# One attention-and-experts kernel: the tail queries' values as five full 128x128 products, and their inverse sums taken after the product

## The chip, the core and the metric

The kernel runs on one core of one Trainium2 chip. The metric is the device time of one execution in microseconds (us). The engines are named as in the profile: PE (matrix products; PEld its weight loads), DVE (VectorE), ACT (ScalarE), POOL (GpSimd) and SP, which issues most DMAs.

## What is computed

Rotary attention over 2 batches, 8 heads, 576 positions and head size 64, whose output feeds a dense mixture of 4 experts (all float32):

```python
q_rot, k_rot = (rotate(q), rotate(k))                 # q, k, v: 2 x 8 x 576 x 64
scores = scale * np.matmul(q_rot, k_rot.transpose(0, 1, 3, 2))
scores = scores - np.max(scores, axis=-1, keepdims=True)
attn = np.exp(scores)
attn = attn / (np.sum(attn, axis=-1, keepdims=True) + 1e-09)
x = np.matmul(attn, v)                                # then to 1152 x 512
for e in range(4):                                    # w1: 512 x 1024, w2: 1024 x 512
    out += p[:, e:e + 1] * (np.maximum(x @ w1[e], 0.0) @ w2[e])
```

## The kernel before

A `Pair` is two heads of one batch. Their 576 queries are 9 blocks: blocks 0 to 3 are the 512 main queries of the first head, 4 to 7 those of the second, and block 8, the **tail**, holds the last 64 queries of both heads, one head under the other on the 128 partitions. Per block the kernel makes scores (line 282), their row maxima (293, DVE), exponentials with row sums (301, ACT), transposes of the exponentials on PE in four pieces of 128 keys (315) and one of the last 64 keys (341), and copies of them out of PSUM.

Main blocks: the transposed exponentials are split into a high and a low float32r part (332 on ACT, 336 on DVE, 344 and 348 for the last keys), multiplied by the split values (365 to 368), and the two halves of the product are added (372 ACT, 376 DVE). When a head pair is complete its inverse sums (382, 383, DVE) are spread over a tile `rep` (392), turned on PE (398), and the product is multiplied by them (403). `out_high` (406, ACT) and `out_low` (410, POOL; DVE for the very last pair) write the two parts that the experts read.

The tail: DVE multiplies all 128x576 exponentials of block 8 by the inverse sums first (387); then come the transposes, ACT copies the four pieces to `at` (351), DVE the last 64 keys (354), and `tail_values` (417) multiplies them by the raw values: for each head five products of 64x64, the last over 64 keys only. ACT (426) and DVE (430) split the result.

The raw values of a pair lie in `rawv` by head (line 159); a pair's load is one DMA for the main rows of both heads (162) and two for the tail rows (170). `split_v` makes the float32r parts. `swap_halves` (first pair only) keeps a copy `lh` of k in the buffer of `at`.

The order of all this work is written as numbers: the dictionaries `ALONE` (first batch, attention alone) and `BESIDE` (second batch, beside the experts) give each step of a block a time in units of blocks, `place` (432) puts it on the agenda, and `plan.run()` issues everything in that order; each engine executes its own list in order. In the first batch there are two sets of buffers and PSUM banks; near its end `narrow` leaves one, and the four pairs of the second batch run between the matmuls of the experts on the first 512 tokens (601 to 603 first layer, 576 to 578 second). Behind them come the experts on the remaining 640 tokens (737 to 739, 822 to 824), whose inputs the `Quarters` steps combine from all pairs' results (644 to 660).

Of the kernel before, what the change touches and what calls it, by code (L numbers as in the profile page):

```python
# [26 lines left out]
    copy_x=2.409, inverse=0.587, scale=0.712, spread=3.143, rows=4.075, divide=4.404, out_high=8.561,  # L27
    out_low=9.259, tail_values=4.354, tail_high=4.658, tail_low=4.771,
# [4 lines left out]
    tail_turn_x=1.122, copy_x=1.44, inverse=0.243, scale=0.697, spread=0.555, rows=2.195, divide=2.503,  # L33
    out_high=9.813, out_low=10.683, tail_values=2.033, tail_high=2.528, tail_low=2.554,
# [21 lines left out]
def kernel(  # L56
# [21 lines left out]
    P = 128  # L78
# [66 lines left out]
    class Pair:  # L145
# [9 lines left out]
        def load(self, s, queue=nc.sync, heads=((0, 2),)):  # L155

            hp, nm = self.hp, self.nm
            src = {"k": k, "q": q, "v": v}[s]
            x = self.pool.tile([P, 2, NS, D], F32, tag=f"raw{s}", name=f"raw{s}{nm}")
            hs = src[self.b, 2 * hp : 2 * hp + 2]  # L160
            for i, (a, z) in enumerate(heads):
                queue.dma_start(
                    out=x[:, a:z, 0:NR, :], in_=hs[a:z, 0:SM, :].rearrange("h (p r) d -> p h r d", r=NR)
                )
                if i:
                    continue
                for j in range(2):
                    rows = slice(j * ST, (j + 1) * ST)
                    if s == "v":
                        queue.dma_start(out=x[rows, :, NR, :], in_=hs[:, SM:S, :].rearrange("h p d -> p h d"))  # L170
                    else:
                        queue.dma_start(out=x[rows, 0, NR, :], in_=hs[j, SM:S, :])
            self.raw[s] = x
# [28 lines left out]
        def split_v(self, eng_h=nc.gpsimd, eng_l=nc.gpsimd):  # L202
            self.vs = self.pool.tile([P, 2, NS, 2, D], F32R, tag="vs", name=f"vs{self.nm}")
            split(eng_h, eng_l, self.raw["v"], self.vs[:, :, :, 0, :], self.vs[:, :, :, 1, :])
# [105 lines left out]
        def turn_e(self, u):  # L310
# [6 lines left out]
            if u == TAIL:  # L317
                self.at = apool.tile([P, NS, P], F32, tag="at", name=f"at{nm}")
# [31 lines left out]
        def copy_e(self):  # L350
            nc.scalar.activation(out=self.at[:, 0:NR, :], in_=self.et.pop(TAIL), func=AF.Copy)

        def copy_x(self):
            nc.vector.tensor_copy(self.at[0:ST, NR, :], px[:, 0:P])
# [46 lines left out]

        def divide(self):
            nc.vector.tensor_tensor(out=self.xf, in0=self.xf, in1=self.pr, op=ALU.mult)
# [4 lines left out]
        def out_low(self):  # L408
            eng = nc.vector if (self.b, self.hp) == (B - 1, NP - 1) else nc.gpsimd
            eng.tensor_tensor(out=self.dst[1], in0=self.xf, in1=f32(self.dst[0]), op=ALU.subtract)  # L410

        def tail_values(self):
            po = self.po = banks["x"].pick()[:, 2 * P : 2 * P + ST]
            for j in range(2):
                for c in range(NS):
                    n = P if c < NR else ST
                    nc.tensor.matmul(  # L417
                        po[j * D : (j + 1) * D, :],
                        lhsT=self.raw["v"][0:n, j, c, :],
                        rhs=self.at[0:n, c, j * ST : (j + 1) * ST],  # L420
                        start=(c == 0),
                        stop=(c == NR),
                    )

        def tail_high(self):
            nc.scalar.activation(out=self.tail_dst[0], in_=self.po, func=AF.Copy)

        def tail_low(self):
            cH, cL = self.tail_dst
            nc.vector.tensor_tensor(out=cL, in0=self.po, in1=f32(cH), op=ALU.subtract)  # L430

        def place(self, u, t, step, o):
# [8 lines left out]
            if u == TAIL:  # L441
                at("tail_turn", self.turn_e, u)
                at("tail_turn_x", self.turn_x, u)
                for key in (
                    "copy_e", "copy_x", "inverse", "scale", "spread", "rows", "divide", "out_high", "out_low",
                    "tail_values", "tail_high", "tail_low",
# [429 lines left out]
    apool = attn.enter_context(tc.tile_pool(name="apool", bufs=1, side="right"))  # L876
    evens, odds = pools("pair")
# [11 lines left out]
    for x in qTt:  # L889
        nc.gpsimd.memset(f32(x), 0.0)  # L890
# [232 lines left out]
```

## Time and profile before

| | |
|---|---|
| three runs, median | 574.27 us (572.32 to 576.47) |
| the profiled execution's own time | 573.63 us |
| its span, first to last instruction | 571.8 us |
| mean granted clock | 0.997 |
| PE, DVE, ACT, POOL busy | 95%, 57%, 49%, 59% of the span |

"Busy" of PE counts pipelined records from start to modelled end, so it doesn't mean full speed. The first batch's attention lies between 8 and 105 us, the second batch's attention beside the experts up to 358, the experts on the last 640 tokens behind that.

### The profile page before, as it was taken

Reading aid. Unit: us, or ns where it says so; the run is one execution under the profiler, and the core shown is the slowest. Engines: PE = TensorE matmul, PEld = TensorE weight load, DVE = VectorE, ACT = ScalarE, POOL = GpSimd, SP = SyncE. Lnnn points to the kernel's source line nnn. Section 1 sums busy time; section 2 is a strip of 40 time slices with the busy share of each in tenths; the row PEclk is TensorE's granted clock in tenths of the full one; section 3 lists DMA queues with packets and bytes.
Section 4 is the critical chain, followed back from the end, with each engine's and each line's share of the span. In section 5 each row is a group of like instructions: output and inputs, shape, how many; then the busy total and the mean of one; then the engine's idle time right before and its main releaser. Section 6 shows DMA issues by size and latency. Waiting matters only on the chain.

```text
span 571.8 us, 8611 instructions
## 1 busy us (share of the span) xinstructions
PE 545.8 (95%) x3229; PEld 478.5 (84%) x3229; DVE 325.4 (57%) x586; ACT 277.8 (49%) x545; POOL 337.5 (59%) x232
## 2 busy tenths in 40 slices
PE   4898988999999999999999998999999999999996
PEld 3788877888888888888888886998899899889985
DVE  5588898234362434444334435995578658757702
ACT  5678888365444544556436552554154225324500
POOL 7999965458824673379244388458663664565400
PEclk9999999899999999999999999999999999999999
DMA  5245023054224222442242222631323213223102
GB/s 151 70 115 136 18 56 97 18 172 153 73 62 156 73 75 54 121 120 70 76 104 79 66 75 76 222 107 38 109 78 100 65 57 111 75 73 78 72 0 92
DMA packets 42459, 50.67 MB, mean 89 GB/s; under 512 B 7218, under 2 KB 32050, under 8 KB 42418
## 3 DMA queue, kind: packets, MB, share of 16 engines
q1 hardware_dynamic: 41618, 49.38, 29.1%
q10 hardware_dynamic: 800, 0.75, 0.5%
q8 instruction: 25, 0.41, 0.3%
q14 instruction: 16, 0.13, 0.1%
HBM read 43.34 MB, written 2.36 MB: 80 GB/s over the span
## 4 chain that ended last, share of the span: by engine, by line
PE 78%; DVE 7%; ACT 7%; POOL 4%; issue 2%; DMA 1%; SPq 0%; ACTq 0%; POOLq 0%; DVEq 0%
PE po L824 6%; PE po L822 6%; PE po L823 6%; PE p L737 6%; PE p L739 5%; PE p L738 5%; PE sc L282 5%; PE ph L601 4%; PE ph L603 4%; PE ph L602 4%; PE po L578 4%; PE po L576 4%; PE po L577 4%; PE pp L315 4%; ACT e L301 3%; PE x L417 3%
## 5 line engine op out<-in xcount | busy, mean ns | idle before, releaser
L142 POOL TENSOR_TENSOR wl<-wr,wh 128x1024 fp32r<-128x1024 f32 x64 | 154.3, 2412 | 145.6 <-ACT wh L135 144.1
L135 ACT ACTIVATE wh<-wr 128x1024 fp32r<-128x1024 f32 x64 | 67.2, 1052 | 28.8 <-PE po L578 16.7
L293 DVE TENSOR_REDUCE mx<-sc 128x1 f32<-128x576 f32 x72 | 54.2, 752 | 37.7 <-PE sc L282 37.3
L301 ACT ACTIVATE e<-sc,mx 128x576 f32<-128x576 f32 x72 | 53.3, 740 | 22.1 <-DVE mx L293 21.6
L142 POOL TENSOR_TENSOR sl<-sf,sh 128x1024 fp32r<-128x1024 f32 x16 | 38.5, 2404 | 42.5 <-ACT sh L135 42.5
L824 PE MATMUL po<-wh,hL 128*128 128x512 f32 x160 | 62.3, 389 | 0.0
L823 PE MATMUL po<-wl,hH 128*128 128x512 f32 x160 | 62.3, 389 | 0.0
L822 PE MATMUL po<-wh,hH 128*128 128x512 f32 x160 | 62.3, 389 | 0.0
L562 DVE SCALAR_TENSOR_TENSOR hL<-ph,hH 128x512 fp32r<-128x512 f32 x32 | 22.1, 692 | 61.1 <-ACT hH L561 61.1
L576 PE MATMUL po<-wh,hH 128*128 128x512 f32 x128 | 52.3, 409 | 0.0
L601 PE MATMUL ph<-xH,wh 128*128 128x512 f32 x128 | 51.5, 402 | 0.0
L315 PE MATMUL pp<-ident,e 128*128 128x128 f32 x288 | 45.3, 281 | 5.9 <-DVE e L387 3.4
L332 ACT ACTIVATE ptH<-pp 128x512 fp32r<-128x512 f32 x64 | 38.1, 595 | 25.1 <-PE x L365 17.3
L578 PE MATMUL po<-wh,hL 128*128 128x512 f32 x128 | 50.3, 393 | 0.0
L336 DVE TENSOR_TENSOR ptL<-pp,ptH 128x512 fp32r<-128x512 f32 x64 | 43.9, 686 | 11.1 <-ACT ptH L332 10.8
L603 PE MATMUL ph<-xH,wl 128*128 128x512 f32 x128 | 50.1, 392 | 0.0
L577 PE MATMUL po<-wl,hH 128*128 128x512 f32 x128 | 50.0, 391 | 0.0
L602 PE MATMUL ph<-xL,wh 128*128 128x512 f32 x128 | 50.0, 391 | 0.0
L135 ACT ACTIVATE sh<-sf 128x1024 fp32r<-128x1024 f32 x16 | 16.9, 1059 | 67.1 <-DVE sf L516 67.1
L775 ACT ACTIVATE hH<-p 128x320 fp32r<-128x320 f32 x64 | 27.1, 435 | 40.3 <-DVE p L767 40.3
L315 PEld LDWEIGHTS pp<-ident,e 128*128 128x128 f32 x288 | 34.3, 143 | 12.2 <-issue 2.0
L516 DVE TENSOR_TENSOR sf<-wr 128x256 f32<-128x256 f32 x30 | 32.2, 1114 | 17.4 <-DMA wr<-in_moe_w_dram 17.4
(164 smaller groups left out, 1375.3 us busy)
## 6 DMA issues: line engine op xcount, KB each, us to landing
wr<-in_moe_w_dram SPq DMA_DIRECT2D x68, 512.0 KB, 3.6
k2T<-kT SPq DMA_DIRECT2D x14, 288.0 KB, 4.1
rawv<-in_v_dram SPq DMA_DIRECT2D x8, 256.0 KB, 3.1
out_dram<-acc SPq DMA_DIRECT2D x8, 256.0 KB, 2.5
rawk<-in_k_dram SPq DMA_DIRECT2D x7, 256.0 KB, 4.1
rawq<-in_q_dram SPq DMA_DIRECT2D x7, 256.0 KB, 3.0
rawv<-in_v_dram SPq DMA_DIRECT2D x16, 32.0 KB, 2.6
tabs<-in_rope_dram ACTq DMA_DIRECT2D x1, 320.0 KB, 3.5
```

The lines of the kernel that those rows point to most:

```text
L135: nc.scalar.activation(out=hi, in_=src, func=AF.Copy)
L142: eng_l.tensor_tensor(out=lo, in0=src, in1=f32(hi), op=ALU.subtract)
L315: nc.tensor.transpose(pp[:, c * P : (c + 1) * P], self.e[u][:, c * P : (c + 1) * P], ident)
L576: nc.tensor.matmul(po[t], lhsT=sH, rhs=wH, start=(f == 0), stop=False)
L577: nc.tensor.matmul(po[t], lhsT=sH, rhs=wL, start=False, stop=False)
L578: nc.tensor.matmul(po[t], lhsT=sL, rhs=wH, start=False, stop=(f == NF - 1))
L601: nc.tensor.matmul(o, lhsT=wH[:, kt], rhs=xh, start=(kt == 0), stop=False)
L602: nc.tensor.matmul(o, lhsT=wH[:, kt], rhs=xl, start=False, stop=False)
L603: nc.tensor.matmul(o, lhsT=wL[:, kt], rhs=xh, start=False, stop=(kt == KT1 - 1))
L822: nc.tensor.matmul(po[t], lhsT=sH, rhs=wH, start=(f == 0), stop=False)
L823: nc.tensor.matmul(po[t], lhsT=sH, rhs=wL, start=False, stop=False)
L824: nc.tensor.matmul(po[t], lhsT=sL, rhs=wH, start=False, stop=(f == NF - 1))
```

## The change

The tail's exponentials are no longer multiplied by the inverse sums. Instead the raw values lie with both heads side by side (`rawv` becomes keys x piece x head x 64), so that one product of 128 value columns by 128 query columns does both heads; of its four 64x64 blocks the two on the diagonal are used. Five such float32 products replace ten. The last one reads `tail_keys`, a 128x128 tile whose lower 64 rows are set to zero once at the start. The tail's inverse sums are turned on PE as a broadcast column (`tail_rows`), ACT keeps the two 64x64 blocks (`keep_tail_rows`), and DVE multiplies the product by them (`tail_divide`). The low part of the tail goes to POOL, as the main part's does. Each load of values is now one DMA per head, with pieces of 64 numbers in SBUF. `lh` moves to another buffer.

```diff
 ALONE = dict(
...
-    copy_x=2.409, inverse=0.587, scale=0.712, spread=3.143, rows=4.075, divide=4.404, out_high=8.561,
-    out_low=9.259, tail_values=4.354, tail_high=4.658, tail_low=4.771,
+    copy_x=2.409, inverse=0.587, spread=3.143, rows=4.075, divide=4.404, out_high=8.561,
+    out_low=9.259, tail_rows=1.6, keep_tail_rows=2.405, tail_values=4.354, tail_divide=4.658, tail_high=4.659, tail_low=4.771,
 )
...
+            if s == "v":
+                x = self.pool.tile([P, NS, 2, D], F32, tag="rawv", name=f"rawv{nm}")
+                for j in range(2):
+                    queue.dma_start(out=x[:, 0:NR, j, :], in_=hs[j, 0:SM, :].rearrange("(p r) d -> p r d", r=NR))
+                for j in range(2):
+                    rows = slice(j * ST, (j + 1) * ST)
+                    queue.dma_start(out=x[rows, NR], in_=hs[:, SM:S, :].rearrange("h p d -> p h d"))
...
-            self.lh = apool.tile([P, NS, P], F32R, tag="at", name=f"lh{self.nm}")
+            self.lh = odds.tile([P, NS, P], F32R, tag="vs", name=f"lh{self.nm}")
...
-            nc.vector.tensor_copy(self.at[0:ST, NR, :], px[:, 0:P])
+            nc.vector.tensor_copy(tail_keys[0:ST], px[:, 0:P])
...
-        def scale(self):
-            e = self.e[TAIL]
-            nc.vector.tensor_scalar_mul(e, e, self.total[:, TAIL:])
...
+        def tail_rows(self):
+            self.prt = xb[1][:, 0:P] if banks["x"].n > 1 else xb[0][:, 3 * P : 4 * P]
+            nc.tensor.transpose(self.prt, self.total[:, TAIL:].to_broadcast([P, P]), ident)
+
+        def keep_tail_rows(self):
+            self.xt = apool.tile([P, ST], F32, tag="xt", name=f"xt{self.nm}", bufs=2)
+            for rows, cols in self.blocks():
+                nc.scalar.activation(out=self.xt[rows], in_=self.prt[rows, cols], func=AF.Copy)
+
+        def blocks(self):
+            return [(slice(j * D, (j + 1) * D), slice(j * ST, (j + 1) * ST)) for j in range(2)]
...
         def tail_values(self):
-            po = self.po = banks["x"].pick()[:, 2 * P : 2 * P + ST]
-            for j in range(2):
-                for c in range(NS):
-                    n = P if c < NR else ST
-                    nc.tensor.matmul(
-                        po[j * D : (j + 1) * D, :],
-                        lhsT=self.raw["v"][0:n, j, c, :],
-                        rhs=self.at[0:n, c, j * ST : (j + 1) * ST],
...
+            po = self.po = banks["x"].pick()[:, 2 * P : 3 * P]
+            for c in range(NS):
+                nc.tensor.matmul(
+                    po,
+                    lhsT=self.raw["v"][:, c].rearrange("p h d -> p (h d)"),
+                    rhs=self.at[:, c, :] if c < NR else tail_keys,
...
+        def tail_divide(self):
+            for rows, cols in self.blocks():
+                nc.vector.tensor_tensor(
+                    out=self.xt[rows], in0=self.po[rows, cols], in1=self.xt[rows], op=ALU.mult
+                )
 
         def tail_high(self):
-            nc.scalar.activation(out=self.tail_dst[0], in_=self.po, func=AF.Copy)
+            nc.scalar.activation(out=self.tail_dst[0], in_=self.xt, func=AF.Copy)
 
         def tail_low(self):
             cH, cL = self.tail_dst
-            nc.vector.tensor_tensor(out=cL, in0=self.po, in1=f32(cH), op=ALU.subtract)
+            self.spare_engine().tensor_tensor(out=cL, in0=self.xt, in1=f32(cH), op=ALU.subtract)
...
+    tail_keys = apool.tile([P, P], F32, name="tail_keys")
...
-    for x in qTt:
+    for x in (*qTt, tail_keys):
         nc.gpsimd.memset(f32(x), 0.0)
```

Two places in the order show what moves. First PE in the last pair of the second batch, between the matmuls of the experts' second layer (`po`); `x_112` and `x_113` are the same PSUM bank, `at` and `tail_keys` the transposed exponentials, `pr` the main rows' inverse sums. Before:

```order
L578 MATMUL po_3_3_3675<-wh_3_1_2_3496,hL_3_5_3567 128x512
L417 MATMUL x_112<-at_3_8_3860,rawv_3_3340 64x64 x10
L398 MATMUL pr_3_3901<-ident,rep_3_3830 128x128 x4
L576 MATMUL po_3_0_3672<-wh_3_1_3_3572,hH_3_6_3608 128x512
L577 MATMUL po_3_0_3672<-wl_3_1_3_3573,hH_3_6_3608 128x512
```

And now, with the changed kernel's own line numbers:

```order
L600 MATMUL po_3_3_3685<-wh_3_1_2_3506,hL_3_5_3577 128x512
L407 MATMUL x_113<-ident,total_3_3399 128x128
L430 MATMUL x_113<-at_3_8_3869,rawv_3_3347 128x128 x4
L430 MATMUL x_113<-tail_keys,rawv_3_3347 128x128
L401 MATMUL pr_3_3909<-ident,rep_3_3840 128x128 x4
L598 MATMUL po_3_0_3682<-wh_3_1_3_3582,hH_3_6_3618 128x512
```

Ten products became five of twice the width, and the transpose of the inverse sums stands in front of them. Second, DVE in the same pair, from the inverse sums to the `Quarters` step (`s`); `xt` is the tail's result. Before:

```order
L383 RECIPROCAL total_3_3389<-total_3_3389 128x9
L348 TENSOR_TENSOR ptX_3_6_3737<-x_112,ptX_3_6_3737 64x256
L392 COPY rep_3_3830<-total_3_3389 128x512
L387 TENSOR_SCALAR e_3_8_3804<-e_3_8_3804,total_3_3389 128x576
L354 COPY at_3_8_3860<-x_112 64x128
L376 TENSOR_TENSOR xf_3_3536<-x_112,tmp_3_3_3869 64x256
L403 TENSOR_TENSOR xf_3_3536<-xf_3_3536,pr_3_3901 128x512
L430 TENSOR_TENSOR xL_76<-x_112,xH_74 128x64
L410 TENSOR_TENSOR xL_76<-xf_3_3536,xH_74 128x512
L644 TENSOR_TENSOR s_3926<-xH_74,xL_76 128x320
```

And now:

```order
L390 RECIPROCAL total_3_3399<-total_3_3399 128x9
L355 TENSOR_TENSOR ptX_3_6_3747<-x_113,ptX_3_6_3747 64x256
L395 COPY rep_3_3840<-total_3_3399 128x512
L361 COPY tail_keys<-x_113 64x128
L383 TENSOR_TENSOR xf_3_3546<-x_113,tmp_3_3_3878 64x256
L418 TENSOR_TENSOR xf_3_3546<-xf_3_3546,pr_3_3909 128x512
L440 TENSOR_TENSOR xt_3_3906<-x_113,xt_3_3906 64x64 x2
L449 TENSOR_TENSOR xL_76<-xt_3_3906,xH_74 128x64
L424 TENSOR_TENSOR xL_76<-xf_3_3546,xH_74 128x512
L666 TENSOR_TENSOR s_3936<-xH_74,xL_76 128x320
```

The multiplication of the exponentials is gone, and two small multiplications stand between the main rows' division and the tail's subtraction.

## Rows read from the trace of the kernel before

**Rows 1.** The page, first part: busy us of PE, its share, instructions; other engines.
```profile
PE 545.8 (95%) x3229; PEld 478.5 (84%) x3229; DVE 325.4 (57%) x586; ACT 277.8 (49%) x545; POOL 337.5 (59%) x232
```
**Rows 2.** Waits of PE: engine, line, what ended the wait: us, times, longest.
```profile
PE pp L315 <- DVE e L387: 3.4, 3, 1.8
PE x L341 <- DVE ptX L348: 1.6, 5, 0.5
```
**Rows 3.** Groups by line: count, busy us, mean ns, idle before.
```profile
L417 PE MATMUL x<-at,rawv 128*64 128x64 f32 (+1 forms) x160 | 15.0, 237 | 0.0
...
L387 DVE TENSOR_SCALAR e<-e,total 128x576 f32<-128x576 f32 x8 | 6.3, 788 | 0.1
```
**Rows 4.** Timeline of PE, last pair's tail: start, us, instruction, count.
```profile
350.69 1.80 PE L417 MATMUL x<-at,rawv 128*64 128x64 f32 x20
...
352.42 0.66 PE L398 MATMUL pr<-ident,rep 128*128 128x128 f32 x4
...
352.83 0.48 PE L576 MATMUL po<-wh,hH 128*128 128x512 f32 x1
```
**Rows 5.** Timeline of PE, float32r transposes of 128x128 in the second batch.
```profile
110.47 0.84 PE L231 MATMUL tpk<-identr,hlk 128*128 128x128 f32 x8
111.15 0.47 PE L601 MATMUL ph<-xH,wh 128*128 128x512 f32 x1
```
**Rows 6.** Timeline, tails of both batches' last pairs; in brackets idle before, and releaser.
```profile
98.55 0.63 PE L315 MATMUL pp<-ident,e 128*128 128x128 f32 x4 [1.40 <-DVE e L387]
...
346.01 1.11 DVE L387 TENSOR_SCALAR e<-e,total 128x576 f32<-128x576 f32 x1
...
347.27 0.63 PE L315 MATMUL pp<-ident,e 128*128 128x128 f32 x4 [1.83 <-DVE e L387]
```
**Rows 7.** The chain that ended last, 98 to 105 us: start, us, what.
```profile
100.46 0.12 PE x L366
...
100.78 0.22 PE x L366
...
102.49 2.31 PE x L417 x20
```
**Rows 8.** Busy us (instructions) by stretch: PE, PEld, DVE, ACT, POOL; clock; DMA.
```profile
20.00:40.00 20.00, 18.39 (x139) 16.61 (x138) 16.64 (x30) 15.94 (x39) 19.09 (x18) 1.00 0.33 88
...
97.00:100.00 3.00, 1.24 (x8) 0.69 (x7) 2.91 (x5) 1.19 (x3) 1.08 (x1) 1.00 0.13 45
100.00:105.00 5.00, 5.00 (x34) 4.30 (x35) 1.56 (x4) 0.54 (x3) 0.00 (x0) 0.66 0.00 0
```
**Rows 9.** Timeline at the experts' start: first product on PE, POOL's subtraction.
```profile
104.74 0.50 PE L601 MATMUL ph<-xH,wh 128*128 128x512 f32 x1
...
105.67 1.29 POOL L410 TENSOR_TENSOR xL<-xf,xH 128x512 fp32r<-128x512 f32 x1 [7.58 <-ACT xH L406]
```
**Rows 10.** Timeline from the last pair's division to the last experts' start.
```profile
353.11 0.69 DVE L403 TENSOR_TENSOR xf<-xf,pr 128x512 f32<-128x512 f32 x1 [3.73 <-PE pr L398]
...
353.72 0.22 DVE L430 TENSOR_TENSOR xL<-x,xH 128x64 fp32r<-128x64 f32 x1
353.83 0.63 ACT L406 ACTIVATE xH<-xf 128x512 fp32r<-128x512 f32 x1 [1.08 <-DVE xf L403]
...
354.50 1.21 DVE L410 TENSOR_TENSOR xL<-xf,xH 128x512 fp32r<-128x512 f32 x1 [0.56 <-ACT xH L406]
...
363.92 0.41 PE L737 MATMUL p<-xH,wh 128*128 128x320 f32 x1 [0.83 <-DVE acc L611]
```
**Rows 11.** Timeline of the start: issue of the first v load, ACT's split of it.
```profile
4.24 0.38 SPq L162 DMA_DIRECT2D rawv<-in_v_dram  x1
...
10.52 0.77 ACT L135 ACTIVATE vs<-rawv 128x640 fp32r<-128x640 f32 x1
```
**Rows 12.** The page: main DMA queue (packets, MB, share); issues (KB, us to landing).
```profile
q1 hardware_dynamic: 41618, 49.38, 29.1%
...
rawv<-in_v_dram SPq DMA_DIRECT2D x8, 256.0 KB, 3.1
```

More of the change, by code (lines that the diff above doesn't have):

```diff
@@ L32 @@
     low_x=1.378, values=2.085, lower=2.576, add=2.643, tail_turn=1.093, copy_e=1.225,
-    tail_turn_x=1.122, copy_x=1.44, inverse=0.243, scale=0.697, spread=0.555, rows=2.195, divide=2.503,
-    out_high=9.813, out_low=10.683, tail_values=2.033, tail_high=2.528, tail_low=2.554,
+    tail_turn_x=1.122, copy_x=1.44, inverse=0.243, spread=0.555, rows=2.195, divide=2.503,
+    out_high=9.813, out_low=10.683, tail_rows=2.032, keep_tail_rows=2.1, tail_values=2.033, tail_divide=2.527, tail_high=2.528,
+    tail_low=2.554,
 )
@@ L158, in load @@
             src = {"k": k, "q": q, "v": v}[s]
+            hs = src[self.b, 2 * hp : 2 * hp + 2]
+            if s == "v":
[5 more added lines that the diff above has]
+                    queue.dma_start(out=x[rows, NR], in_=hs[:, SM:S, :].rearrange("h p d -> p h d"))
+                self.raw[s] = x
+                return
             x = self.pool.tile([P, 2, NS, D], F32, tag=f"raw{s}", name=f"raw{s}{nm}")
-            hs = src[self.b, 2 * hp : 2 * hp + 2]
             for i, (a, z) in enumerate(heads):
@@ L167, in load @@
                 for j in range(2):
[L168 to L172, printed above, removed]
+                    queue.dma_start(out=x[j * ST : (j + 1) * ST, 0, NR, :], in_=hs[j, SM:S, :])
             self.raw[s] = x
@@ L203, in split_v @@
             self.vs = self.pool.tile([P, 2, NS, 2, D], F32R, tag="vs", name=f"vs{self.nm}")
-            split(eng_h, eng_l, self.raw["v"], self.vs[:, :, :, 0, :], self.vs[:, :, :, 1, :])
+            by_head = self.raw["v"].rearrange("p c h d -> p h c d")
+            split(eng_h, eng_l, by_head, self.vs[:, :, :, 0, :], self.vs[:, :, :, 1, :])
         def turn(self, which, i):
@@ L317, in turn_e @@
             if u == TAIL:
-                self.at = apool.tile([P, NS, P], F32, tag="at", name=f"at{nm}")
+                self.at = apool.tile([P, NR, P], F32, tag="at", name=f"at{nm}")
             elif u % 2 == 0:
@@ L408, in out_low, with spare_engine @@
         def out_low(self):
-            eng = nc.vector if (self.b, self.hp) == (B - 1, NP - 1) else nc.gpsimd
-            eng.tensor_tensor(out=self.dst[1], in0=self.xf, in1=f32(self.dst[0]), op=ALU.subtract)
+            self.spare_engine().tensor_tensor(out=self.dst[1], in0=self.xf, in1=f32(self.dst[0]), op=ALU.subtract)
         def tail_values(self):
-            po = self.po = banks["x"].pick()[:, 2 * P : 2 * P + ST]
-            for j in range(2):
-                for c in range(NS):
-                    n = P if c < NR else ST
-                    nc.tensor.matmul(
-                        po[j * D : (j + 1) * D, :],
-                        lhsT=self.raw["v"][0:n, j, c, :],
-                        rhs=self.at[0:n, c, j * ST : (j + 1) * ST],
-                        start=(c == 0),
-                        stop=(c == NR),
-                    )
+            po = self.po = banks["x"].pick()[:, 2 * P : 3 * P]
[4 more added lines that the diff above has]
+                    rhs=self.at[:, c, :] if c < NR else tail_keys,
+                    start=(c == 0),
+                    stop=(c == NR),
+                )
[3 more added lines that the diff above has]
+                    out=self.xt[rows], in0=self.po[rows, cols], in1=self.xt[rows], op=ALU.mult
+                )
         def tail_high(self):
-            nc.scalar.activation(out=self.tail_dst[0], in_=self.po, func=AF.Copy)
+            nc.scalar.activation(out=self.tail_dst[0], in_=self.xt, func=AF.Copy)
         def tail_low(self):
             cH, cL = self.tail_dst
-            nc.vector.tensor_tensor(out=cL, in0=self.po, in1=f32(cH), op=ALU.subtract)
+            self.spare_engine().tensor_tensor(out=cL, in0=self.xt, in1=f32(cH), op=ALU.subtract)
+        def spare_engine(self):
+            return nc.vector if (self.b, self.hp) == (B - 1, NP - 1) else nc.gpsimd
         def place(self, u, t, step, o):
@@ L444, in place @@
                 for key in (
-                    "copy_e", "copy_x", "inverse", "scale", "spread", "rows", "divide", "out_high", "out_low",
-                    "tail_values", "tail_high", "tail_low",
+                    "copy_e", "copy_x", "inverse", "spread", "rows", "divide", "out_high", "out_low", "tail_rows", "keep_tail_rows",
+                    "tail_values", "tail_divide", "tail_high", "tail_low",
                 ):
```

2 lines of the change are left out of this document (1 added, 1 removed).

## Prediction

> **What bounds the kernel now.** I read the page's busy shares first: the reader is to see TensorE (PE) busy for 545.8 of 571.8 us, far ahead of the other engines [rows 1]. So whatever goes from PE's own list of work, or from its idle time, counts. Then I read what PE's idle time waits for: the costliest releaser inside the program, apart from the one wait at the very start, is the multiplication of the tail's exponentials by the inverse sums (line 387), 3.4 us in three waits; beside it five waits for the ptX subtraction (line 348) [rows 2]. Third, the groups by line: the tail's product (line 417) is 160 records, 20 for each of 8 pairs [rows 3]. Last, the timeline around single tails, the chain and the granted clock. All sums are made against the profiled execution, 573.63 us; the median of the three runs is 574.27, 0.6 higher. A difference of about 1% (5.7 us) is what a measurement of this kernel can tell from none.
>
> **The product on PE.** Before, ten 64x64 float32 products per pair are 20 records, because each such product leaves two. In the last pair they occupy PE from 350.69 to 352.42, 1.73 us or 0.087 each, and PE is never idle there [rows 4]. After, five products are 10 records with 128 weight columns and 128 moving columns. The trace has no ordinary 128x128 float32 product, so I bound one record. From below: the eight float32r transposes of the same size take (111.15 - 110.47) / 8 = 0.085 us each [rows 5]. They move half as much as I expect here, and yet are no faster than the 64-column records; so 0.085 looks like a floor under any pair of load and product, and the old records like 64-column work standing on that floor. From above: if a record's cost goes with its columns, 2 x 0.087 = 0.173. The nearest row is the float32 transpose of 128x128: four go by in 352.83 - 352.42 = 0.41, 0.10 each, or 0.11 with the first one's lead [rows 4]. I take 0.11: 10 x 0.11 = 1.1 us. The change adds one more float32 transpose per pair (the inverse sums), 0.1 us. A pair gains 1.73 - 1.1 - 0.1 = 0.53 us of PE.
>
> In the second batch PE has no other limit, so its four pairs give 4 x 0.53 = **-2.1 us**. In the first batch the four engines are close together: from 20 to 40 us PE is busy 18.4, POOL 19.1, VectorE (DVE) 16.6 and ScalarE (ACT) 15.9 of 20 [rows 8], and the next product waits for a subtraction, an exponential and a copy that the change delays (below). Its first three pairs give between 0 and 0.53; I take 0.25: **-0.8 us**. Pair 3 is counted with the clock.
>
> **The stall at the multiplication.** The tail's transposes need the scaled exponentials today. After the change they need only the exponentials, which are ready earlier. In the last pair PE stands 1.83 us until a 1.11 us multiplication is done [rows 6]. Nothing takes its place at once, for the inverse sums are now wanted only by a transpose that stands behind the remaining expert products of that step: **-1.83 us**. In pair 3 of the first batch PE stands 1.40 us [rows 6]. What is late next there is the chain of DVE's subtractions ptL and ptX, which stands behind the multiplication in DVE's order and moves up with it; I count **-1.3**. In the first three pairs DVE gets back 0.79 us each [rows 3]; the five waits for ptX, 1.6 us [rows 2], should shrink, but pair 3's has been counted and ACT is close behind: **-0.8**, between 0 and -1.8.
>
> **The clock.** From 97 to 100 PE is busy 1.24 of 3 us. In the next 5 us the mean granted clock is 0.66, so for some 3.4 of them the lower level (1.2 GHz) was granted instead of 2.4 [rows 8]. In the chain five records of the value product then take up to 0.22 instead of 0.12 (0.5 us in all), and the 20 records of the tail's product take 2.31 us instead of 1.73 [rows 7]. If the idle time goes, I expect the clock to stay up: -0.5 for the five, and 2.31 - 1.2 = -1.1 for the product with its transpose. With the stall, pair 3 gives 1.3 + 0.5 + 1.1 = **-2.9 us**.
>
> **What the change adds to two chains.** The product by the inverse sums (two 64x64 multiplications on DVE) now stands between the tail's product and the high part on ACT, and the high part of the main rows is queued behind it on ACT. A DVE operation on 128x64 takes 0.22 us [rows 10]; two, with the ACT copy's 0.2 behind them, are 0.65 to 0.7. (1) At the start of the experts the first products on pair 3's own rows come nine matmuls after 104.74, and POOL's subtraction ends at 105.67 + 1.29 = 106.96 [rows 9], when PE just wants it. ACT's high part comes 0.7 later against the end of the tail's product and the tail's subtraction, now on POOL, about 0.25 ahead of it; the main multiplication no longer needs to be waited for. PE then waits 0.4: **+0.4**. (2) In the last pair DVE runs from line 403 through 430 and 410 and the quarters' sums to the expert sums, for which PE waits 0.83 at 363.92 already [rows 10]. Everything from the tail on shifts by the two multiplications and ACT's wait: **+0.7**.
>
> **Costed at nothing.** The two ACT copies of the transposed sums lie in front of the next exponential, which in the first batch waits for DVE anyway; if that cover is gone they cost 0.4 per pair, which is inside the term for the first batch. The extra memset on POOL lies before the first load lands. The swapped copy of k only changes its buffer. POOL's tail subtraction elsewhere waits on work done long before.
>
> **The loads of v.** Each head is now a DMA of its own, and its pieces in SBUF are 256 B instead of 1 KB. One load of the old kind lands 3.1 us after issue [rows 12]; the first is issued at 4.24 and read by ACT at 10.52 [rows 11], a slack of about 3.2. All packets of the main queue average 0.291 x 16 x 571.8 / 41618 = 64 ns [rows 12]. If a 256-byte packet cost as much, a load has 48 packets more per DMA engine, 3.1 us, plus 0.4 for the second issue: 3.5 us, just over the slack. I take 0.
> The Trainium skill ("DMA: Bandwidth & Descriptors", Specifications) puts the smallest transfer at full rate at 512 bytes, which speaks against these pieces; no run here shows a large load in 256-byte pieces yet.
>
> **Sum.** -2.1 - 0.8 - 1.83 - 0.8 - 2.9 + 0.4 + 0.7 = -7.3 us. From the profiled execution 566.3, from the median 567.0: **566.7 us**.
>
> **Rivals.**
> *The clock falls all the same and the first batch gives nothing* (chance 0.20). For it: PE still has to wait for DVE and ACT in pair 3. Against it: the longest idle piece goes. Pair 3 keeps 1.3 of stall, loses 0.1 (ten records at twice 0.11 and the transpose at 0.2 are 2.4 against 2.31) and 0.4; the first three pairs pay 0.1 each for the transpose: -1.3 + 0.1 + 0.4 + 0.3 - 2.1 - 1.83 + 0.7 = -3.7, **570.2 us**.
> *A record costs as its columns*, 0.173 (0.07). Then the product gains nothing and the transpose costs 0.1: seven pairs +0.7, pair 3 -1.3 - 0.5 - 0.5 + 0.4, the stall -1.83, DVE -0.8, the chain +0.7: -3.1, **570.8 us**.
> *Ordinary float32 products stream four times slower than transposes* (0.03). Then a product costs 0.44 and five 2.2 us, 0.57 more per pair with the transpose: 7 x 0.57 = 4.0, pair 3 -1.4, the rest -1.9: +0.7, **574.6 us**. Against it: the 64-column records would take at least 0.11, and take 0.087 [rows 4].
> The Trainium skill ("TensorE: Matmul & The Clock Gate", Terms) says that the transpose mode is four times faster for FP32; by that rule a transpose is no measure for a product, and the time is this rival's. The trace so far doesn't agree with it, by the 0.087.
> *Slower: the load of the weights no longer hides* (0.04). Place: the ten records, which now fill all 128 columns of the array, each accumulating on the one before. If they stood one behind another, each would cost what a float32 transpose costs alone, 0.66 - 3 x 0.11 = 0.33 [rows 4]: 3.3 + 0.1 - 1.73 = 1.67 more per pair, 11.7 in seven, pair 3 -0.3, the rest -1.9: +9.5, **583.5 us**. It turns slower from 0.21 per record (80 x r = 17.0). Against it: the old records accumulate too, and overlap.
> *The first v load comes late* (0.06): ACT's split waits, POOL's work behind it shifts, and POOL, busy 19.1 of 20 us from 20 on [rows 8], has no reserve. Late by 0.3 to 2 us: with 2 us **568.7**.
>
> **How the numbers follow.** The forecast has 0.60, the rivals 0.20, 0.07, 0.03, 0.04 and 0.06. Faster by over 1% means under 568.5: nearly all of the forecast's share, half of the late load's and a little of the others': 0.62. Slower: 0.04. The rest, 0.34, is within 1%. The range reaches down to 562.5 (first batch in full, -1.6 more for the products and the waits, no cost in the two chains, -1.1, a little more relief on DVE) and up to 571.5, above the first two rivals.
>
> **What would show it.** Right: the tail's product 10 records per pair at 0.11; no wait of the tail's transposes for DVE; the clock from 100 to 105 near 1; the wait near 363 longer than 0.83 by some 0.7; a short new wait for POOL's subtraction at the experts' start. Wrong: records at 0.17 or more, a low clock in another place, ACT waiting for a v load.

## The result, and the profile after

| | before | after |
|---|---|---|
| median, us | 574.27 (572.32 to 576.63, 7 runs) | 568.35 (568.11 to 570.07, 7 runs) |
| ratio, 95% interval | | 0.9907 (0.9882 to 0.9933) |
| the profiled execution: time, span | 573.63, 571.8 | 568.24, 566.5 |

The kernel became 0.9% faster, some 5.3 us by the ratio. A second comparison, below, gave 0.9931 (0.9907 to 0.9956). The forecast was 7.3 us. The profile of the changed kernel shows most of the expected gains, and two losses. First the page's busy time, the waits of PE, and the groups of the tail's product (columns as in [rows 1 to 3]):

```profile
PE 540.3 (95%) x3157; PEld 475.5 (84%) x3157; DVE 323.5 (57%) x587; ACT 281.3 (50%) x561; POOL 339.0 (60%) x240
```
```profile
PE p L759 <- DVE acc L633: 2.5, 2, 1.7
...
PE x L372 <- ACT xt L412: 0.6, 1, 0.6
...
PE ph L624 <- POOL xL L424: 0.5, 1, 0.5
```
```profile
L430 PE MATMUL x<-at,rawv 128*128 128x128 f32 x64 | 8.6, 277 | 0.0
L430 PE MATMUL x<-tail_keys,rawv 128*128 128x128 f32 x16 | 3.1, 275 | 0.0
```

The three waits for the multiplication [rows 2] are gone. Two others are new, 0.6 us for ScalarE's copies in pair 3 and 0.5 for GpSimd at the experts' start, and the one for the expert sums grew. And the product is 80 records instead of 160 [rows 3]. The duration of a record overlaps the next one's, so the cost of one is read from starts. The timeline of PE at the last pair's tail answers to [rows 4]:

```profile
343.74 0.27 PE L407 MATMUL x<-ident,total 128*128 128x128 f32 x1
343.85 1.06 PE L430 MATMUL x<-at,rawv 128*128 128x128 f32 x8
344.75 0.39 PE L430 MATMUL x<-tail_keys,rawv 128*128 128x128 f32 x2
344.97 0.60 PE L401 MATMUL pr<-ident,rep 128*128 128x128 f32 x4
```

Ten records take 344.97 - 343.85 = 1.12 us, 0.112 each; the transpose in front takes 0.11. What is new lies on VectorE behind it. Its timeline in the last pair, GpSimd's beside it, and PE's two waits at the end of the chain (they answer to [rows 10]):

```profile
345.61 0.69 DVE L418 TENSOR_TENSOR xf<-xf,pr 128x512 f32<-128x512 f32 x1 [3.08 <-PE pr L401]
346.55 0.46 DVE L440 TENSOR_TENSOR xt<-x,xt 64x64 f32<-64x64 f32 x2 [0.26 <-ACT xt L412]
347.33 1.27 DVE L449 TENSOR_TENSOR xL<-xt,xH 128x64 fp32r<-128x64 f32 x1 [0.32 <-ACT xH L445]
348.53 1.38 DVE L424 TENSOR_TENSOR xL<-xf,xH 128x512 fp32r<-128x512 f32 x1
```
```profile
346.12 2.40 POOL L143 TENSOR_TENSOR wl<-wr,wh 128x1024 fp32r<-128x1024 f32 x1 [1.53 <-ACT wh L136]
348.47 0.89 POOL L682 TENSOR_TENSOR t1L<-s,t1H 128x320 fp32r<-128x320 f32 x1
```
```profile
356.27 0.42 PE L759 MATMUL p<-xH,wh 128*128 128x320 f32 x1 [1.70 <-DVE acc L633]
...
358.25 0.42 PE L759 MATMUL p<-xH,wh 128*128 128x320 f32 x1 [0.83 <-DVE acc L633]
```

The subtraction in line 449 handles 64 columns in 1.27 us; the same step before took 0.22, with its start at 353.72 [rows 10] inside a GpSimd operation of the same kind:

```profile
351.93 2.39 POOL L142 TENSOR_TENSOR wl<-wr,wh 128x1024 fp32r<-128x1024 f32 x1 [2.31 <-ACT wh L135]
```

Now it ends at 348.60, just behind GpSimd's operation, which ends at 346.12 + 2.40 = 348.52. The next one ends at 349.91, 0.55 behind GpSimd's next operation (348.47 + 0.89). Both read two operands from SBUF; the step before the change had one in PSUM. From line 418's start to the end of line 424 are 4.30 us; before, 2.60. PE's waits grew by the same 1.7, from 0.83 to 2.53.

The windows answer to [rows 8] (us, busy by engine, clock, DMA):

```profile
18.00:24.00 6.00, 5.59 (x24) 5.24 (x25) 3.22 (x6) 3.86 (x10) 5.67 (x6) 0.50 0.21 52
97.00:100.00 3.00, 2.15 (x15) 1.77 (x16) 1.47 (x5) 1.19 (x5) 0.50 (x1) 1.00 0.04 11
100.00:105.00 5.00, 4.54 (x26) 3.63 (x25) 1.46 (x4) 1.17 (x4) 1.60 (x2) 1.00 0.00 0
355.00:358.00 3.00, 1.14 (x6) 0.89 (x6) 2.97 (x6) 2.10 (x5) 2.25 (x1) 1.00 0.75 280
```

The clock stays up at 100 to 105 us, as forecast, but from 18 to 24 us it is at the lower level (1.2 GHz); the last section shows that the kernel before ran at that level there too, until some 22 us. The following table gives the spans between marks on PE (the starts of the tail's products T0 to T7, of the experts E and of the last experts Q), worked out from the timelines of the profiled executions:

| us | to T0 | T0-T2 | T2-E | E-T4 | T4-T6 | T6-T7 | T7-Q | Q-end |
|---|---|---|---|---|---|---|---|---|
| before | 41.23 | 42.73 | 20.78 | 68.82 | 116.52 | 60.61 | 7.70 | 213.4 |
| after | 41.65 | 41.97 | 17.46 | 69.66 | 115.17 | 57.94 | 7.04 | 215.6 |
| v_pieces_alone | 41.29 | 43.15 | 19.31 | 68.97 | 116.54 | 60.64 | 7.71 | 213.5 |
| product_alone | 41.22 | 40.61 | 20.37 | 69.36 | 115.04 | 59.91 | 7.03 | 214.1 |
| move_alone | 41.28 | 41.97 | 18.51 | 69.44 | 116.69 | 58.72 | 7.70 | 216.3 |
| no_scale | 41.40 | 41.69 | 18.00 | 68.84 | 116.51 | 58.63 | 7.71 | 214.2 |
| after_again | 41.87 | 42.27 | 17.51 | 69.68 | 115.17 | 57.96 | 7.04 | 217.0 |
| best1 | 40.95 | 41.96 | 17.95 | 69.24 | 115.18 | 59.17 | 6.60 | 213.7 |

Up to Q the changed kernel is 7.5 us ahead (358.39 against 350.89); 2.2 of it go behind Q.

### The profile page after: what moved, and what is told of

Read it like the earlier page. It is cut to its first block, busy times and chain, and to the rows that moved or that the text cites. A ratio compares the mean times of both kernels' runs of the same rounds, so it can differ in the third digit from the quotient of the medians.

```text
span 566.5 us, 8507 instructions
## 1 busy us (share of the span) xinstructions
PE 540.3 (95%) x3157; PEld 475.5 (84%) x3157; DVE 323.5 (57%) x587; ACT 281.3 (50%) x561; POOL 339.0 (60%) x240
## 3 DMA queue, kind: packets, MB, share of 16 engines
q1 hardware_dynamic: 47890, 49.38, 29.6%
## 4 chain that ended last, share of the span: by engine, by line
PE 76%; ACT 7%; DVE 6%; POOL 5%; DMA 3%; issue 2%; SPq 1%; ACTq 0%; POOLq 0%; DVEq 0%
PE po L846 6%; PE po L845 6%; PE po L844 6%; PE p L759 6%; PE p L760 6%; PE p L761 6%; PE sc L289 5%; PE ph L624 4%; PE ph L625 4%; PE ph L623 4%; PE po L600 4%; PE po L598 4%; PE po L599 4%; PE pp L322 3%; ACT e L308 3%; PE x L372 2%
```

## The experiments

My theory after the result: the product and the vanished stalls gave what was forecast, and the tail's new chain on VectorE in the last pair took more back. The rival: one of the two halves of the change gave little, since other engines are late at the same places.

**product_alone and move_alone**, one half of the change each. The first takes the transpose, the copies and the multiplications behind the product out again and scales the exponentials; the second keeps ten 64x64 products:

```diff
+            nc.vector.tensor_scalar_mul(e, e, self.total[:, TAIL:])
...
-            self.spare_engine().tensor_tensor(out=cL, in0=self.xt, in1=f32(cH), op=ALU.subtract)
+            for rows, cols in self.blocks():
+                nc.vector.tensor_tensor(out=cL[rows], in0=self.po[rows, cols], in1=f32(cH)[rows], op=ALU.subtract)
```
```diff
+            for j, (rows, cols) in enumerate(self.blocks()):
...
+                        po[rows, cols],
+                        lhsT=self.raw["v"][0:n, c, j, :],
+                        rhs=self.at[:, c, cols] if c < NR else tail_keys[0:n, cols],
```

> The five 128x128 products alone: the exponentials are multiplied by the inverse sums first, as before the change, and the inverse sums' transpose and the two multiplications behind the product are not there; the values lie side by side. Ten records at 0.112 instead of twenty at 0.087 are 0.61 us less per pair. Theory A: in the first batch TensorE isn't what the end waits for, so only the second batch's four pairs count: -2.4, and +0.2 for the last pair's halves that VectorE and ScalarE now handle in two pieces: -2.2 from before, 572.1. Theory B: the first batch's pairs gain in full: another -1.8 to -2.3, 570.0. In both the wait of the tail's transposes for the multiplication stays (3.4 us in the whole kernel, 1.8 in the last pair), and the low clock from 100 to 105 us stays.

> The inverse sums behind the product alone: all of the change, but the tail's values are ten 64x64 products (twenty records) as before. Theory A, the sum that I now hold: -1.83 (wait in the last pair), -1.3 - 0.5 - 0.6 (pair 3 of the first batch, with the clock up from 100 to 105), +0.4 (the transpose in the second batch's four pairs), +0.4 (wait for GpSimd at the experts' start), +1.7 (the longer chain of the last pair): -1.7 from before, 572.6; with VectorE's relief in the first batch counted too, -2.5, 571.8. Theory B: the removed multiplication is worth more than its waits, since it holds VectorE for 0.8 us in front of each tail: -4 or more, 570 or less. The rise of the clock shows in both: 100 to 105 us near 1.0.

Measured: product_alone 568.82 us, ratio 0.9927 (0.9903 to 0.9950), -4.2 us; move_alone 572.07, ratio 0.9968 (0.9949 to 0.9988), -1.8. The two add up to -6.0, near the whole change's -5.3. So the product gave more than its own 1.2 us in the first batch (T0 to T2 is 2.1 shorter), and the move gave its stalls less what its own steps cost: in move_alone the span behind Q is 2.9 longer than before (a fall of the clock at 361 us is in it). Two thirds of the gain are the product's, a third is the move's. The low clock expected of product_alone at the end of the first batch did come (next experiment).

**v_pieces_alone**: the kernel before with the new layout and loads of v; the product reads `self.raw["v"][0:n, c, j, :]`.

> The kernel before, with the values loaded as in the changed kernel (a DMA per head, 256-byte pieces in SBUF) and nothing else changed; the products stay 64x64. Theory A: a load still lands about 3 us after its issue and nothing waits for it: 574.3, within 0.6 of before. Theory B: the pieces cost, at the start (ScalarE's first split of the values waits) or later by holding up the weights' loads: 575.5 or more.

Measured: 572.66 us, ratio 0.9993 (0.9978 to 1.0008). A load lands 3.0 us after issue, in twice the pieces:

```profile
q1 hardware_dynamic: 47890, 49.38, 29.1%
...
rawv<-in_v_dram SPq DMA_DIRECT2D x16, 128.0 KB, 3.0
```

Theory A. This profile tells something else, since its tail work is that of before [rows 8]:

```profile
97.00:100.00 3.00, 1.27 (x10) 0.86 (x9) 2.89 (x6) 1.39 (x4) 1.55 (x1) 1.00 0.24 84
100.00:105.00 5.00, 4.97 (x39) 4.14 (x40) 2.22 (x6) 1.43 (x4) 0.32 (x1) 1.00 0.00 0
```

PE idles as much from 97 to 100 us as before, and the clock stays up; T2 to E is 1.5 us shorter (19.31 against 20.78). But product_alone, which keeps the multiplication and the wait for it too, has the fall again:

```profile
97.00:100.00 3.00, 2.64 (x14) 2.21 (x13) 1.51 (x5) 0.60 (x1) 0.00 (x0) 0.70 0.00 0
100.00:105.00 5.00, 4.73 (x25) 3.98 (x23) 1.55 (x4) 1.46 (x4) 1.29 (x1) 0.84 0.00 0
```

So the low clock came in two of the three profiled executions that keep this wait, and in none of the eleven without it. It goes with the wait, but not every execution pays it, and so few profiles don't tell how often.

**double_first**: the tail's products issued twice in the first three pairs (`for c in [*range(NS)] * 2`).

> The changed kernel, with the tail's five products issued twice in the first three pairs of the first batch (the first round's result is thrown away): 10 more records of 0.112 us each, 1.12 us more of TensorE per pair. Theory A: TensorE sets the pace there, so the product's gain in the first batch was real and full: +3.4, 571.8. Theory B: other engines set it and TensorE has room: less than +1.0, 568.4 to 569.3.

Measured: 573.0 us, ratio 0.9979 (0.9955 to 1.0004): +4.1 us against the changed kernel's 0.9907, +2.8 against its 0.9931, for 3.4 us of work. In the profiled execution (571.25 us) T0 lies at 41.04 and E at 103.32: 62.28 us between them, 2.85 more than in the changed kernel. Theory A: PE sets the pace there.

**no_scale**: `scale` does nothing in the kernel before.

> The kernel before without the multiplication of the tail's exponentials by the inverse sums: that part of the computation is left out (the tail's values are not divided), and nothing stands in its place, so the added steps of the change (transpose, copies, two multiplications, GpSimd's subtraction) are missing too. Theory A: the stalls' part of the sum was right: -1.8 (last pair), -1.3 and -1.1 for pair 3 of the first batch with the clock up (0.5 for the value product, 0.6 for the tail's twenty records), up to -0.8 for VectorE's relief: -4.2 to -5.0 from before (573.3), 568.3 to 569.1. The inverse sums' move alone then gave only some -1.5 because the added steps took 2.5 to 3 us back. Theory B: the stalls were worth less, since other engines are late at the same places: -2 or less, 571.3 or more; then the added steps cost little.

Measured: 569.46 us, ratio 0.9936 (0.9917 to 0.9955), -3.7 us. 0.5 short of A, whose lower end lies inside the interval (-2.6 to -4.8); B lies outside. The stall in the last pair is worth 60.61 - 58.63 = 2.0 us, pair 3's 19.31 - 18.00 = 1.3 when the profile of v_pieces_alone stands for before, and 2.8 against the profile of before, whose clock fell. How much of the clock's 1.6 comes on average, the time doesn't tell. Against move_alone (-1.8), the added steps of the change cost some 2 us.

**last_in_psum**: the last pair's divided tail goes to PSUM.

```diff
+            last = self.spare_engine() is nc.vector
+            to = self.po[:, 0:ST] if last else self.xt
...
-                    out=self.xt[rows], in0=self.po[rows, cols], in1=self.xt[rows], op=ALU.mult
+                    out=to[rows], in0=self.po[rows, cols], in1=self.xt[rows], op=ALU.mult
...
+            self.xt = to
```

> The changed kernel, with one edit: in the very last pair the two small multiplications write their result into PSUM, so that VectorE's subtraction for the tail's low part reads one operand from PSUM and one from SBUF, as it did before the change. Theory A: in the changed kernel this subtraction (128x64, 1.27 us) spent some 1.05 us waiting for the GpSimd operation then running, because both its operands lie in SBUF. Then it takes 0.2 to 0.3 us here. The main rows' subtraction behind it still has both operands in SBUF and has to wait for the same GpSimd operation to end (about 0.75 us after it is ready); if it goes ahead of GpSimd's next operation, the chain is 0.8 us shorter, TensorE's two waits for the expert sums fall from 2.5 to 1.7 us, and the time is 567.5 (0.8 less than 568.35); if GpSimd goes first, nothing is won. Theory B: the subtraction is slow for another reason (its place behind the small multiplications, the copy that ran on ScalarE at the same time). Then it still takes about 1.2 us and the time is the changed kernel's, 568.3.

Measured: 568.95 us, ratio 0.9930 (0.9909 to 0.9952): no gain to be seen in the time. On VectorE the mechanism is A's:

```profile
344.64 0.69 DVE L418 TENSOR_TENSOR xf<-xf,pr 128x512 f32<-128x512 f32 x1 [3.07 <-PE pr L401]
345.58 0.50 DVE L442 TENSOR_TENSOR x<-x,xt 64x64 f32<-64x64 f32 x2 [0.25 <-ACT xt L412]
346.37 0.23 DVE L452 TENSOR_TENSOR xL<-x,xH 128x64 fp32r<-128x64 f32 x1 [0.29 <-ACT xH L448]
346.89 1.22 DVE L424 TENSOR_TENSOR xL<-xf,xH 128x512 fp32r<-128x512 f32 x1 [0.29 <-ACT xH L421]
```
```profile
345.15 2.40 POOL L143 TENSOR_TENSOR wl<-wr,wh 128x1024 fp32r<-128x1024 f32 x1 [1.53 <-ACT wh L136]
347.51 1.33 POOL L685 TENSOR_TENSOR t1L<-s,t1H 128x320 fp32r<-128x320 f32 x1
```

The subtraction takes 0.23 instead of 1.27, with GpSimd at the same operation throughout, and lines 418 to 424 take 348.11 - 344.64 = 3.47 us, 0.83 less. But GpSimd's next operation then takes 1.33 instead of 0.89, two of VectorE's quarters' sums behind it take 0.99 instead of 0.85 and 0.92 instead of 0.49, so that 0.4 of the 0.8 is lost by the last `acc`; and the 2.1 us of waits that are left were followed by a fall of the clock in this execution (third column from the right):

```profile
355.00:358.00 3.00, 2.17 (x10) 1.91 (x11) 2.97 (x7) 0.74 (x3) 1.90 (x1) 0.75 0.98 371
358.00:361.00 3.00, 3.00 (x17) 3.00 (x16) 2.49 (x6) 1.88 (x4) 1.46 (x1) 0.68 0.63 236
```

**main_first and low_on_dve**: both keep an edit of last_in_psum; main_first moves the main rows' parts ahead of the tail's in pair 3, low_on_dve puts the tail's subtraction on VectorE, from PSUM, in all pairs.

```diff
-            pr.place(u, n + u, 1, ALONE)
+            pr.place(u, n + u, 1, dict(ALONE, **({}, dict(out_high=4.405, out_low=4.7))[hp == NP - 1]))
```

> The changed kernel with the PSUM edit of the last pair, and in pair 3 of the first batch the main rows' high and low part go ahead of the tail's on ScalarE and GpSimd. Theory A: TensorE's wait of 0.46 us for GpSimd's subtraction at the experts' start comes only from the tail's steps in front of it (0.5 to 0.6 us on the two engines together); it goes, nothing takes its place, and the time is 568.5, 0.45 under the version with the PSUM edit alone (568.95). Theory B: the next product waits for the weights' parts or the exponentials instead: 568.95.

> The changed kernel with the tail's low part back on VectorE in all eight pairs, the divided tail kept in PSUM. Theory A: GpSimd, busy over 90% of the time from 20 to 40 us, is what the first batch waits for in the end, so that the subtraction that the change gave it (0.3 us for each pair) took back part of what the product gave; from the first to the third tail's product the time falls by 0.6 us or more against the changed kernel, the wait for GpSimd at the experts' start goes: 567.6. Theory B: GpSimd's extra work is hidden and VectorE's is not: 568.9 to 569.4.

Measured: 568.05 us (ratio 0.9902, 0.9873 to 0.9930) and 567.57 (0.9899, 0.9870 to 0.9927). In main_first GpSimd begins with the main rows, and PE has no wait in the first 5 us of the experts (busy 5.00 from 100 to 105, against 4.54):

```profile
102.45 1.29 POOL L424 TENSOR_TENSOR xL<-xf,xH 128x512 fp32r<-128x512 f32 x1 [4.76 <-ACT xH L421]
103.69 0.32 POOL L452 TENSOR_TENSOR xL<-xt,xH 128x64 fp32r<-128x64 f32 x1
```

The 0.46 us is shown by that, not by the time, whose intervals overlap. For low_on_dve theory A's time came, but not its signs in the trace: T0 to T2 is 42.0 us, as after, and the wait for GpSimd at the experts' start is still there (0.66 us), since ScalarE's order kept the tail in front. Whether GpSimd's 0.3 per pair matters stays open.

**rows_first**: last_in_psum, and in the last pair both kinds of inverse sums turned one step earlier, the main rows ahead of the tail.

> The changed kernel with the PSUM edit of the last pair, and that pair's order changed: the transposes of both kinds of inverse sums come one step of the experts earlier, and the main rows' division, high and low part go ahead of the tail's on every engine. Theory A: what the changed kernel loses behind the last pair is VectorE's chain (subtractions that wait for GpSimd, in an order that meets GpSimd's longest operation), the 2.1 to 2.5 us that TensorE idles for the expert sums at its end, and in some executions a fall of the clock behind this idle time. By the trace the first of the quarters' sums on VectorE should start some 3 us earlier against the tail's product, TensorE's waits fall under 0.6 us (plus 0.3 for the spread sums at the earlier transposes), and the granted clock stays at 1.0 from 355 to 365 us: 566.0 to 566.5, about 2.5 under the version with the PSUM edit alone (568.95). Theory B: something else arrives just then (the weights' parts from GpSimd and ScalarE, or a load), and takes the place of the wait: 568 or more.

Measured: 568.35 us, ratio 0.9912 (0.9880 to 0.9943). The waits for the expert sums fell to 0.21 and 0.83, but theory B's kind of wait took their place, at 342 us: the tail's transpose goes to the PSUM bank that VectorE's add still reads.

```profile
342.24 0.32 PE L407 MATMUL x<-ident,total 128*128 128x128 f32 x1 [1.43 <-DVE xf L383]
```

**after_again, best0, best1**: the changed kernel once more, and two versions that collect the edits. best0 is low_on_dve with main_first's order and the last pair's two copies on VectorE; best1 adds, for the last pair:

```diff
-dict(out_high=2.55, out_low=2.6))[hp])
+dict(spread=0.3, rows=1.75, divide=1.7505, out_high=1.751, out_low=1.7515))[hp])
```

> The changed kernel itself once more, for its spread and a second profile. If the low clock from 17 to 24 us that its first profile shows belongs to the change, it is there again at the same place; if it is a matter of the single execution, it is missing or elsewhere (then the first tail's product starts at about 40.9 instead of 41.65). Time 568.4.

> Three edits of the runs so far together: the tail's low part on VectorE from PSUM in all pairs (567.57 alone), the main rows' parts ahead of the tail's in pair 3 of the first batch (568.05 with the PSUM edit of the last pair), and the two copies of the turned inverse sums in the last pair on VectorE, which idles there, instead of behind a long copy on ScalarE. Theory A (the gains add): 0.4 for the wait of 0.46 at the experts' start, 0.25 for the wait for the copies: 566.9. Theory B: the wait for the expert sums at 355 to 358 us doesn't move, because VectorE's chain meets GpSimd's operation there in any case: 567.5.

> As best0, and in the last pair the spread copy of the inverse sums goes ahead of the ptX subtraction, and the main rows' inverse sums are turned, divided and split one step of the experts earlier (the tail's transpose stays where it was, so that TensorE needn't wait for the add that cost 1.43 us in the version with both earlier). Theory A: TensorE waits about 0.6 us for ScalarE's copy of the tail's exponentials before the earlier transposes, but VectorE reaches the quarters' sums about 2.8 us earlier against the tail's product, and of the 2.1 us of waits for the expert sums under 0.5 is left: 566.0, 1 under best0. Theory B: the earlier transposes lose at 341 us what is won at 356: as best0.

Measured: after_again 570.12 us (566.52 to 570.63), ratio 0.9931; best0 567.80, ratio 0.9910 (0.9888 to 0.9932); best1 567.01 us (565.45 to 567.89), ratio 0.9892 (0.9872 to 0.9912), the lowest of all, though its interval overlaps the changed kernel's. For best0 the time decides nothing; the wait at the experts' start is gone, as both theories have it, and the wait for the expert sums, 1.3 us at 356, didn't move, which is B. best1 does what was expected of it: PE waits 0.58 at the earlier transposes, and of the waits for the sums only one is left. The spread copy starts 0.25 us ahead of GpSimd's operation and takes 0.43 us:

```profile
341.09 0.66 PE L401 MATMUL pr<-ident,rep 128*128 128x128 f32 x4 [0.58 <-ACT at L358]
356.81 0.41 PE L764 MATMUL p<-xH,wh 128*128 128x320 f32 x1 [0.83 <-DVE acc L638]
```
```profile
337.68 0.43 DVE L395 COPY rep<-total 128x512 f32<-128x512 f32 x1
...
337.93 2.42 POOL L143 TENSOR_TENSOR wl<-wr,wh 128x1024 fp32r<-128x1024 f32 x1 [0.56 <-ACT wh L136]
```

In the changed kernel it starts 0.66 us behind the start of that operation and ends 0.28 behind its end:

```profile
339.24 2.00 DVE L395 COPY rep<-total 128x512 f32<-128x512 f32 x1
...
338.58 2.38 POOL L143 TENSOR_TENSOR wl<-wr,wh 128x1024 fp32r<-128x1024 f32 x1 [0.58 <-ACT wh L136]
```

The second profile of the changed kernel has the low clock from 17 to 24 us again, and a fall behind the waits that the first hadn't:

```profile
18.00:24.00 6.00, 5.47 (x25) 4.78 (x23) 3.13 (x5) 3.89 (x11) 5.67 (x7) 0.50 0.24 55
...
355.00:358.00 3.00, 1.30 (x8) 0.89 (x6) 2.97 (x6) 2.71 (x6) 1.64 (x1) 1.00 0.83 222
358.00:361.00 3.00, 2.17 (x9) 2.15 (x9) 2.71 (x8) 0.65 (x1) 0.73 (x1) 0.60 0.84 316
```

The later fall costs 217.0 - 215.6 = 1.4 us. As for the early one, seven of the eleven profiles of the changed kernel and its variants show it, and none of the three of the kernel before and its variants (its own, v_pieces_alone, no_scale). best1 and last_in_psum, whose first 40 us of code are the changed kernel's but for where the divided tail lies, don't. So it belongs to the execution; whether the changed kernel falls into it more often than before isn't settled. It costs little: T0 lies between 40.6 and 42.1 us in the seven profiles that show it, and between 40.9 and 41.4 in the other seven.

## Why the prediction was right, and where its sum was off

The direction, the mechanism and the range (562.5 to 571.5) held; the sum of -7.3 us was 2 too large. By its steps:

- **The product in the second batch, -2.1.** Right: 0.112 us per record against 0.11 taken, and T4 to T6 is 1.35 shorter for two pairs, 0.67 each against 0.53. The rivals with 0.173, 0.22 and 0.33 per record fall. By the Trainium skill's rule ("TensorE: Matmul & The Clock Gate", Terms), read as that rival reads it, a product was to cost four transposes; the trace doesn't agree: a record of the product starts 0.112 us after the last, a float32 transpose 0.09 to 0.11 (ten records make five products, so a whole product is 0.22, twice a transpose).
- **The product in the first batch, -0.8.** Undersized for the product alone: double_first shows that PE sets the pace there, and product_alone gained 2.1 us from T0 to T2. I had taken a quarter of a microsecond per pair because four engines are nearly equally busy; equal busy shares don't say which one is waited for.
- **The stall in the last pair, -1.83.** Right: T6 to T7 is 2.67 shorter, 0.67 of it the product's.
- **VectorE's relief in the first batch, -0.8.** Right alone (T0 to T2 in move_alone and no_scale 0.8 to 1.0 shorter), but it doesn't add to the product's gain: both together give 0.8 there in the profile of the changed kernel (best1 the same), product_alone 2.1. What the added steps take back there was not found.
- **Pair 3, -2.9.** T2 to E is 3.3 shorter against the profiled execution, but only 1.85 against v_pieces_alone. The 1.6 us for the clock were real in that profile and are not part of each execution with the wait. One step that failed: a fall of the clock in the one profiled execution was priced as if every run paid it. Another is a term put at nothing: the 1.40 us stall is gone, but PE now waits 0.6 in pair 3 for the two ACT copies of the turned sums. In turn "a low clock in another place", named there as a sign against the forecast, did come: from 17 to 24 us, where the kernel before was at the lower level for most of the time too, and in the second profile behind 358 us.
- **GpSimd at the experts' start, +0.4.** Right: 0.46 us, and main_first removes it. (E to T4 grew by 0.84 us in all; main_first's 69.03 takes 0.63 of it back.)
- **The last pair's chain, +0.7.** What was priced was right, but a term was missing, and with what follows this is the largest miss in the profiles: +1.7. The two multiplications and the copy behind them took about what was priced (in last_in_psum, where the subtraction is short again, the chain is 0.87 longer than before); the step that failed is the subtraction, for whose move to two SBUF operands the sum had no term: it took 1.27 instead of 0.22, since GpSimd was at work. last_in_psum shows that the operand's place does it. Behind it come 0.5 that the waits don't explain (0.35 of it after PE's last record, from whose start to the end of the span are 5.32 us instead of 4.97), and in some executions 1.4 for the clock.
- **The loads, 0.** Right, and the rival of the late load falls: ACT's first split starts at 10.26 without a wait, and the packets of the main queue take 29.1% of its engines' time in both kernels, for 47890 as for 41618 packets [rows 12]. The swapped copy of k costs nothing in its other buffer either: product_alone, which has it, reaches T0 at 41.22, the kernel before at 41.23.
The Trainium skill ("DMA: Bandwidth & Descriptors", Specifications) speaks against pieces under 512 bytes; the trace doesn't show the cost: 3.0 us to landing for 128 KB in 256-byte pieces, and 572.66 against 573.21 us.

## What to carry to other kernels

A step that moves an operand from PSUM to SBUF can change its price without changing its shape: look what GpSimd does at that time, and count a VectorE operation on two SBUF operands to the end of GpSimd's running one. A fall of the clock that one profile shows may come in some executions only; look at a second profile, and price it with a chance, not in full. And where several engines are about equally busy, add work to one of them and see who pays, before a gain on it is halved.

## What was not expected of the hardware

- VectorE's subtraction of 128x64 takes 0.22 or 0.23 us with one operand in PSUM, and 1.27 with both in SBUF while GpSimd runs a 2.40 us operation on SBUF; it ends 0.08 behind that operation. The 0.22 and 0.23 were taken beside such an operation too. A copy of 128x512 from SBUF to SBUF takes 0.43 when it starts ahead of GpSimd's operation (best1), and 2.00 when it starts behind. Who waits first goes first, as far as these rows show: in last_in_psum VectorE stood ready and went ahead at 347.5, and GpSimd's next operation took 1.33 instead of 0.89.
The Trainium skill ("SBUF — State Buffer", Who interferes with whom) has this as an exclusive lock of a shared pair of ports, for VectorE operations with two SBUF inputs and, under conditions, for copies; the trace agrees, by the 1.27 and the 2.00.
- The granted clock fell in three places, each only in some executions: between 17 and 25 us, between 98 and 104 us, and between 356 and 365 us, each time during or behind TensorE's idle time. The mean granted clock of a run doesn't order the times, though: of the 23 runs of before beside the first four experiments, the five with 0.998 or more took 571.98 to 572.75 us, the seven with 0.993 or 0.994 took 571.99 to 573.45, the nine with 0.996 or 0.997 took 573.21 to 576.03, and the two with 0.991 took 575.87 and 575.99. Where in those runs the clock was low isn't known.
- The timeline of PE in the profile of before, scores of two blocks, and behind it two in the changed kernel:

```profile
20.93 0.83 PE L282 MATMUL sc<-kT,qT 128*128 128x288 f32 x2
...
22.60 0.51 PE L282 MATMUL sc<-kT,qT 128*128 128x288 f32 x2
```
```profile
14.76 0.54 PE L289 MATMUL sc<-kT,qT 128*128 128x288 f32 x2 [0.42 <-ACT e L308]
...
20.46 0.83 PE L289 MATMUL sc<-kT,qT 128*128 128x288 f32 x2
```

In the changed kernel two records take 0.83 us at 20.46, where the window from 18 to 24 us gives the clock as 0.50, and 0.54 at 14.76, ahead of the fall. The kernel before has 0.83 at 20.93 and 0.51 at 22.60, though the windows give its clock as 1.00 at both times: it too was at the lower level until some 22 us, and at the start of a span that column alone doesn't show it. So the early fall of the changed kernel mainly took back a rise that had come earlier than in the kernel before.
